# Cached attention decode on one core: two-head units of B against four-head units

## The chip, the cores and the metric

The kernel runs on one NeuronCore of one Trainium2 chip. The metric is the device time of one execution in microseconds (us). The kernel before took 248.0 us, the median of three runs that lie between 247.71 and 248.01. The core has a matrix engine (PE, with its weight loads shown as PEld), a vector engine (DVE), a scalar engine (ACT), a general engine (POOL), a sync engine (SP, which here only issues DMA transfers), and 16 DMA engines that bring data from HBM into the on-chip SBUF.

## The reference

Two independent decode steps, A and B, are computed and concatenated. Each has one query token, 32 query heads, 16 key/value heads of 128 elements and a cache of 8192 positions. A looks at the last 2048 positions alone, B at all of them. All inputs are bf16.

```python
def _B_ref(x, k_cache, v_cache, wq, wo):
    q = (x @ wq).reshape(1, 1, 32, 128).transpose(0, 2, 1, 3)
    k = jnp.repeat(k_cache, 2, axis=1)
    v = jnp.repeat(v_cache, 2, axis=1)
    scores = jnp.einsum("bhqd,bhkd->bhqk", q, k) * (128 ** -0.5)
    p = _softmax(scores, axis=-1)
    o = jnp.einsum("bhqk,bhkd->bhqd", p, v)
    return o.transpose(0, 2, 1, 3).reshape(1, 1, 4096) @ wo
```

A is the same with `k_cache[:, :, 6144:, :]` and `v_cache[:, :, 6144:, :]`. Each cache value is used once, so the work is mostly the reading of some 103 MB.

## The kernel before

**Units.** The heads are worked off in units: four units of four key/value heads for A (numbers 0 to 3), then eight units of two heads for B (numbers 4 to 11). K or V of a unit of A is one transfer of 2048 KB (128 rows of 16 KB, one row for each SBUF partition); of a unit of B it is one transfer of 4096 KB (128 rows of 32 KB). A unit's data is cut into slabs of 2048 elements for each partition, 4 slabs in A and 8 in B.

**The ring.** All large loads go through one SBUF buffer, `ring`, of 72 K elements for each partition. `place` gives each load the next free stretch, starts again at 0 where the load does not fit before the end, and makes the transfer wait for the last user of whatever lay there. A K transfer is last used by the transpose of its last slab (`T<unit>.<slab>`), a V transfer by the last product with it (`V<unit>.<slab>`). All these transfers are issued by SP, in this order and one after the other: the two wq, then K0, K1, V0, K2, V1 and so on (K is one unit ahead of V), and at the end wo of A and wo of B, the latter in six pieces that grow smaller. A transfer that waits holds up all that stand behind it in SP's program.

**A slab of K** is transposed on DVE (`turn`, L368, into one of three buffers `ktb`) and multiplied on PE with the query (`score`, L385, four matmuls), which adds up a PSUM bank of scores for the unit.

**The softmax of a unit** is a chain over engines: `peak` (maximum on DVE, L400, turned on PE, L402), `spread` (maximum over each head on DVE, and its return to all partitions by a matmul on PE, L425), `expo` (a copy on DVE, L431, and the exponential on ACT, L434), `turnp` (the transposes of the result on DVE, L442 for A and L446 for B).

**The product with V** is `pv` (L461), four matmuls of a slab that write to different row groups of one PSUM bank; `take` copies the bank out on ACT, and `fold` (L477) adds the parts on PE.

**Order.** Each engine has its own list, and the order in it is written out: the loop at L485 puts the slabs of unit i+1 (`ahead`) between the steps of the softmax of unit i. In B the last four of the eight slabs of unit i+1 stand between the products of unit i, one slab after every second product. After the loop come the row sums, the division and the product with wo (L544), whose pieces wait for the pieces of wo.

Of the kernel before, what the change touches and what calls it, by code (L numbers as in the profile page):

```python
# [5 lines left out]
F32 = mybir.dt.float32  # L6
# [106 lines left out]
def bass_concat_heads__sliding_block_cached__gqa_block_cached__decode_kernel(nc, A_x, A_k_cache, A_v_cache, A_wq, A_wo,  # L113
# [19 lines left out]
    zb = nc.alloc_sbuf_tensor("zb", [128, NP, 4, ZW], BF16)  # L133
# [6 lines left out]
    mr = nc.alloc_sbuf_tensor("mr", [128, 32], F32)  # L140
    mexpa = nc.alloc_sbuf_tensor("mexpa", [1, 128], F32)
# [4 lines left out]
    mexp = nc.alloc_sbuf_tensor("mexp", [128, 128], F32)  # L146
# [3 lines left out]
    pts = nc.alloc_sbuf_tensor("pts", [128, 16, 16, 2, 2], BF16)  # L150
    rsall = nc.alloc_sbuf_tensor("rsall", [128, NP], F32)
    cls = nc.alloc_sbuf_tensor("cls", [128, 4], F32)
# [65 lines left out]
    kv_at = {}  # L218

    def load_a(kind, u):  # L220
        c = (ks if kind == "K" else vs)[0]
        src = bass.AP(tensor=c.tensor, offset=c.offset + (4 * u * SK + SK - W_A) * DH,
                      ap=[[TA * DH, 32], [SK * DH, 4], [1, TA * DH]])
        kv_at[kind, "A", u] = place(TA * DH, ["T%d.%d" % (u, NA - 1) if kind == "K" else "V%d.%d" % (u, NA - 1)],
                                    lambda e, t: e.dma_start(t, src), "%s%d" % (kind, u))

    def load_b(kind, p):
        c = (ks if kind == "K" else vs)[1]
        src = c[0, 2 * p:2 * p + 2, :, :].rearrange("h (q t) d -> (h q) (t d)", q=64)
        i = NQ + p  # L230
        kv_at[kind, "B", p] = place(ROW, ["T%d.%d" % (i, NB - 1) if kind == "K" else "V%d.%d" % (i, NB - 1)],
                                    lambda e, t: e.dma_start(t, src), "%s%d" % (kind, i))

    UNITS = [("A", u) for u in range(NQ)] + [("B", p) for p in range(NP)]
    NU = len(UNITS)
    for i in range(NU + 1):
        for kind, n in (("K", i), ("V", i - 1)):
            if 0 <= n < NU:
                side, u = UNITS[n]
                (load_a if side == "A" else load_b)(kind, u)  # L240
# [10 lines left out]
    def slab(kind, side, u, s):  # L251
        return kv_at[kind, side, u][:, s * SLAB:(s + 1) * SLAB]
# [9 lines left out]
    op("pool", lambda e: e.memset(mexp[:], 0.0), name="mexp0")  # L262
# [33 lines left out]
    op("dve", lambda e: e.memset(vb[0][:, :], 0.0), name="vb0.0")  # L296
    for h in range(2):
        op("dve", lambda e, h=h: e.tensor_reduce(
            cls[:, 2 * h:2 * h + 2], view(identf, 128, 64 * h, [[1, 2], [32, 2], [2, NB]]), AX.XY, ALU.add),
            deps=["identf"], name="clsB%d" % h)  # L300
# [12 lines left out]
    for P in range(2):  # L313
# [24 lines left out]
        srcs = [[512, NP], [64, 2], [1, 2], [128, 2]]  # L338
        for b in range(4):
            if P == 1:  # L340
                op("dve", lambda e, b=b: e.tensor_copy(
                    view(zb, NP * 4 * ZW, 32 * b + W0, [[4 * ZW, NP], [2 * ZW, 2], [ZW, 2], [1, 2]], 32, 32 * b),
                    view(ktb, KT, b // 2 * 256, srcs, 32, 32 * b)),
                    deps=["qT%d" % u for u in range(8, 16)] + ["zb0"], name="z1.%d" % b)
# [9 lines left out]
    nslab = [NA if side == "A" else NB for side, _ in UNITS]  # L354
# [9 lines left out]
    def turn(i, s):  # L364
        side, u = UNITS[i]
        k = k0[i] + s
        kt, src = ktb[:, (k % NKT) * SLAB:(k % NKT + 1) * SLAB], slab("K", side, u, s)
        op("dve", lambda e: e.transpose(kt.bitcast(I32), src.bitcast(I32)),  # L368
           deps=["K%d" % i] + (["S%d" % (k - NKT)] if k >= NKT else Z), name="T%d.%d" % (i, s))
# [35 lines left out]
    def spread(i):  # L405
        side, _ = UNITS[i]
        deps = ["mT%d" % i, "mexp0"] + (["mx%d" % (i - 1), "bc%d" % (i - 1)] if i else [])
        if side == "A":
            op("dve", lambda e: e.tensor_reduce(mr[0:1, 8:16], view(mb, 512, 0, [[1, 8], [8, 16]], parts=1),
                                                AX.X, ALU.max), deps=deps, name="mr%d" % i)  # L410
            op("dve", lambda e: e.tensor_scalar(
                mexpa[:].rearrange("p (a m) -> p a m", m=8), view(mr, 32, 8, [[0, 16], [1, 8]], parts=1), -SCALE, None,
                ALU.mult), deps=["mr%d" % i], name="mx%d" % i)
        else:
            for h in range(2):
                op("dve", lambda e, h=h: e.tensor_reduce(
                    mr[0:1, 2 * h:2 * h + 2], view(mb, 512, 64 * h, [[1, 2], [32, 2], [2, NB]], parts=1), AX.XY, ALU.max),
                    deps=deps, name="mr%d" % i if h else None)
            for h in range(2):
                op("dve", lambda e, h=h: e.tensor_scalar(  # L420
                    view(mexp, 128, 64 * h, [[32, 2], [2, NB], [1, 2]], parts=1),
                    view(mr, 32, 2 * h, [[0, 2], [0, NB], [1, 2]], parts=1), -SCALE, None, ALU.mult),
                    deps=["mr%d" % i], name="mx%d" % i if h else None)
        row = mexpa if side == "A" else mexp
        op("pe", lambda e: e.matmul(mb[:, 128:129], lhsT=row[0:1, :], rhs=onesf[0:1, 0:1], start=True, stop=True),  # L425
           deps=["mx%d" % i, "ones"], name="bc%d" % i)

    def expo(i):
        side, u = UNITS[i]
        c = i % 2  # L430
        op("dve", lambda e: e.tensor_copy(nb[:, c:c + 1], mb[:, 128:129]),  # L431
           deps=["bc%d" % i] + (["exp%d" % (i - 2)] if i >= 2 else []), name="nb%d" % i)
        acc = (rsa if side == "A" else rsall)[:, u:u + 1]
        op("act", lambda e: e.activation(psb[:, :], sbank[i][:, :], ACT.Exp, bias=nb[:, c:c + 1], scale=SCALE,  # L434
                                         accum_out=acc),
           deps=["nb%d" % i, "warm1"] + (["PT%d" % (i - 1)] if i else []), name="exp%d" % i)

    def turnp(i):
        side, _ = UNITS[i]
        deps = ["exp%d" % i, "pts0"] + (["V%d.%d" % (i - 1, nslab[i - 1] - 1)] if i else [])  # L440
        if side == "A":
            op("dve", lambda e: e.transpose(view(pta, NA * 128, 0, [[8, 16], [128, NA], [1, 8]]), psb[:, :]),  # L442
               deps=deps, name="PT%d" % i)
        else:
            for h in range(2):
                op("dve", lambda e, h=h: e.transpose(  # L446
                    view(pts, 1024, 2 * h, [[4, 16], [64, 16], [1, 2]], 64, 64 * h), psb[64 * h:64 * h + 64, :]),
                   deps=deps, name="PT%d" % i if h else None)

    def pv(i, s):  # L450
        side, u = UNITS[i]

        def mm(e):
            src = slab("V", side, u, s)
            for j in range(4):
                if side == "A":
                    lhsT = pta[:, s, 4 * j:4 * j + 4, :].rearrange("p t k -> p (t k)")
                else:
                    lhsT = view(pts, 1024, 64 * s + 16 * j, [[1, 16]])
                n = 32 if side == "A" else 16  # L460
                ins = e.matmul(vbank[i][32 * j:32 * j + n, :], lhsT=lhsT, rhs=src[:, 512 * j:512 * j + 512],  # L461
                               start=(s == 0), stop=(s == nslab[i] - 1))
            return ins
        op("pe", mm, deps=["V%d" % i, "PT%d" % i, "vb0.0"] + (["xo%d" % (i - 1)] if i else []), name="V%d.%d" % (i, s))
# [20 lines left out]
    for i in range(NU):  # L485
# [34 lines left out]
        lsel[:, 1, :].rearrange("p (g c) -> p g c", c=4), rsall[:, :].unsqueeze(2).to_broadcast([128, NP, 4]),  # L520
        view(cls, 4, 0, [[0, NP], [1, 4]]), ALU.mult), deps=["exp%d" % last, "clsB0", "clsB1"], name="lsel")
# [68 lines left out]
```

## Time and profile before

| what | value |
|---|---|
| median of three runs | 248.0 us (247.71 to 248.01) |
| the profiled execution | 247.88 us |
| its span, first to last instruction | 246.1 us |
| PE busy | 182.6 us (74%) |
| DVE busy | 146.0 us (59%) |
| ACT busy | 23.6 us (10%) |
| read from HBM | 102.76 MB, 418 GB/s over the span |
| mean granted PE clock | 0.826 of full |

The span is what the profile shows; the device time is 1.78 us longer in the profiled execution. Busy shares are means over the whole span. The DMA rows of the page give the mean busy share of the 16 DMA engines in 40 slices of 6.15 us and the rate at which they moved data.

### The profile page before, as it was taken

The page shows a single profiled execution, that of the slowest core. Times are in us where ns is not written, and L with a number is a line of the kernel's source. Part 1 is how long each engine was busy: PE and PEld are TensorE (multiplying, and loading weights), DVE is VectorE, ACT ScalarE, POOL GpSimd, SP SyncE. Part 2 cuts the span into 40 slices and gives each one's busy share as a digit, 9 for nine tenths or more (in the row PEclk, how much of TensorE's full clock was granted, in tenths as well). Part 3 has the DMA queues.
Part 4 walks back from the last instruction along what each step waited for, and adds up shares of the span by engine and source line. Part 5 has one row for each costly group of instructions (what it writes and reads, how often), then busy time and mean ns, then how long its engine had stood idle before and what let it go on. Part 6 is the DMA issues. An engine that isn't in the chain of part 4 may idle for free.

```text
span 246.1 us, 2421 instructions
## 1 busy us (share of the span) xinstructions
PE 182.6 (74%) x1009; PEld 75.8 (31%) x1009; DVE 146.0 (59%) x224; ACT 23.6 (10%) x48; POOL 1.8 (1%) x12
## 2 busy tenths in 40 slices
PE   1169857789868787878759849939949939985695
PEld 0024322234423241252142224215215205231562
DVE  2467877577688687259449447656736826932200
ACT  2002110021111010000001001001001001011000
POOL 2000000000000000000000000000000000000000
PEclk9999995787999977968976965985895985795589
DMA  7999999999999999999999999999999999999993
GB/s 261 423 440 421 442 426 419 426 429 471 426 418 437 426 426 426 423 431 431 431 442 439 431 426 437 442 423 422 426 426 426 437 434 426 431 432 461 389 400 139
DMA packets 5058, 102.91 MB, mean 418 GB/s; under 512 B 564, under 2 KB 824, under 8 KB 1336
## 3 DMA queue, kind: packets, MB, share of 16 engines
q1 hardware_dynamic: 5044, 102.77, 97.8%
q8 instruction: 8, 0.13, 0.2%
q10 hardware_dynamic: 4, 0.00, 0.0%
q14 instruction: 2, 0.02, 0.0%
HBM read 102.76 MB, written 0.00 MB: 418 GB/s over the span
## 4 chain that ended last, share of the span: by engine, by line
DMA 57%; PE 22%; DVE 16%; issue 2%; SPq 1%; ACT 0%; DVEq 0%
DMA ring<-in_B_k_cache_dram 31%; DVE ktb L368 13%; DMA ring<-in_B_v_cache_dram 10%; DMA ring<-in_B_wo_dram 10%; PE qb L385 6%; DMA ring<-in_A_wq_dram 5%; PE sb L324 4%; PE sb L385 4%; PE qb L324 3%; PE ob L477 2%; DVE pts L446 2%; PE mb L425 1%; SPq L247 1%; PE qb L377 1%; PE vb L461 0%
## 5 line engine op out<-in xcount | busy, mean ns | idle before, releaser
L368 DVE STREAM_TRANSPOSE ktb<-ring 128x1024 int32<-128x1024 int32 x80 | 95.3, 1221 | 16.4 <-DMA ring<-in_B_k_cache_dram 13.8
L385 PE MATMUL sb<-ktb,zb 128*128 128x512 bf16 x256 | 83.1, 462 | 25.4 <-DVE ktb L368 25.4
L385 PEld LDWEIGHTS sb<-ktb,zb 128*128 128x128 bf16 x256 | 23.0, 108 | 75.5 <-DVE ktb L368 42.3
L461 PE MATMUL vb<-ring,pts 128*16 128x512 bf16 x256 | 21.1, 420 | 3.9 <-DVE pts L446 2.6
L385 PE MATMUL qb<-ktb,za 128*128 128x512 bf16 x64 | 21.5, 488 | 1.5 <-DVE ktb L368 1.5
L477 PEld LDWEIGHTS ob<-sel,xo 128*128 128x128 f32 x96 | 18.5, 272 | 4.5 <-issue 1.6
L400 DVE TENSOR_REDUCE mx<-sb 128x1 f32<-128x512 f32 x8 | 5.5, 691 | 22.9 <-PE sb L385 22.9
L477 PE MATMUL ob<-sel,xo 128*128 128x4 f32 (+1 forms) x96 | 16.9, 301 | 0.7 <-ACT xo L468 0.7
L468 ACT ACTIVATE xo<-vb 128x512 f32<-128x512 f32 x12 | 7.2, 597 | 91.9 <-PE vb L461 91.9
L324 PE MATMUL sb<-ring,xrep 128*128 128x512 bf16 x40 | 10.6, 418 | 6.6 <-DMA ring<-in_A_wq_dram 5.7
L431 DVE COPY nb<-mb 128x1 f32<-128x1 f32 x12 | 1.9, 159 | 18.2 <-PE mb L425 18.2
L544 PE MATMUL qb<-ring,oP 128*1 128x320 bf16 (+1 forms) x128 | 10.8, 318 | 1.4 <-DMA ring<-in_A_wo_dram 0.7
L446 DVE STREAM_TRANSPOSE pts<-psb 64x512 bf16<-64x512 bf16 x16 | 11.0, 688 | 1.0 <-ACT psb L434 0.8
L434 ACT ACTIVATE psb<-sb,nb 128x512 bf16<-128x512 f32 x8 | 5.5, 687 | 61.1 <-DVE nb L431 61.1
L385 PEld LDWEIGHTS qb<-ktb,za 128*128 128x128 bf16 x64 | 6.4, 115 | 13.8 <-issue 7.0
L335 DVE STREAM_TRANSPOSE ktb<-qsb 128x256 int32<-128x256 int32 x16 | 7.1, 445 | 5.6 <-ACT qsb L330 5.3
L461 PEld LDWEIGHTS vb<-ring,pts 128*16 128x16 bf16 x256 | 4.1, 91 | 18.4 <-issue 15.3
L402 PE MATMUL mb<-identf,mx 128*1 128x128 f32 x24 | 4.6, 271 | 7.0 <-DVE mx L400 7.0
L324 PE MATMUL qb<-ring,xrep 128*128 128x512 bf16 x40 | 9.3, 379 | 0.0
L544 PEld LDWEIGHTS qb<-ring,oP 128*1 128x1 bf16 x128 | 6.6, 90 | 5.5 <-DMA ring<-in_B_wo_dram 2.2
L324 PEld LDWEIGHTS sb<-ring,xrep 128*128 128x128 bf16 x40 | 4.1, 105 | 12.6 <-issue 9.0
L554 DVE CAST outsb<-qb 1x256 bf16<-1x256 f32 x2 | 0.8, 421 | 11.5 <-PE qb L544 11.5
(73 smaller groups left out, 71.5 us busy)
## 6 DMA issues: line engine op xcount, KB each, us to landing
ring<-in_B_k_cache_dram SPq DMA_DIRECT2D x8, 4096.0 KB, 25.2
ring<-in_B_v_cache_dram SPq DMA_DIRECT2D x8, 4096.0 KB, 32.2
ring<-in_A_k_cache_dram SPq DMA_DIRECT2D x4, 2048.0 KB, 31.5
ring<-in_A_v_cache_dram SPq DMA_DIRECT2D x4, 2048.0 KB, 26.8
ring<-in_A_wo_dram SPq DMA_DIRECT2D x1, 4608.0 KB, 16.6
ring<-in_A_wq_dram SPq DMA_DIRECT2D x1, 4096.0 KB, 12.6
ring<-in_B_wq_dram SPq DMA_DIRECT2D x1, 4096.0 KB, 22.6
ring<-in_B_wo_dram SPq DMA_DIRECT2D x1, 2304.0 KB, 21.8
```

The costliest lines, as they stand in the source:

```text
L324: ins = e.matmul(bank[:, :], lhsT=lhsT, rhs=o, start=(k == 0), stop=(k == 4))
L335: op("dve", lambda e, n=n: e.transpose(ktb[:, n * 512:(n + 1) * 512].bitcast(I32), qsb[:, n % 2, :].bitcast(I32)), deps=["qe%d" % u] + ([" ...
L368: op("dve", lambda e: e.transpose(kt.bitcast(I32), src.bitcast(I32)), deps=["K%d" % i] + (["S%d" % (k - NKT)] if k >= NKT else Z), name="T ...
L385: ins = e.matmul(bank[:, :], lhsT=lhsT, rhs=view(ktb, KT, (k % NKT) * SLAB + 64 * c + v, [[128, 16], [2, 32]]), start=(side == "B" and s = ...
L400: op("dve", lambda e: e.tensor_reduce(mx[:, 0:1], sbank[i][:, :], AX.X, ALU.max), deps=["S%d" % (k0[i] + nslab[i] - 1)] + (["mT%d" % (i - ...
L402: op("pe", lambda e: e.matmul(mb[0:1, 0:128], lhsT=mx[:, 0:1], rhs=identf[:, :], start=True, stop=True), deps=["max%d" % i] + was, name="m ...
L434: op("act", lambda e: e.activation(psb[:, :], sbank[i][:, :], ACT.Exp, bias=nb[:, c:c + 1], scale=SCALE, accum_out=acc), deps=["nb%d" % i, ...
L446: op("dve", lambda e, h=h: e.transpose(view(pts, 1024, 2 * h, [[4, 16], [64, 16], [1, 2]], 64, 64 * h), psb[64 * h:64 * h + 64, :]), deps= ...
L461: ins = e.matmul(vbank[i][32 * j:32 * j + n, :], lhsT=lhsT, rhs=src[:, 512 * j:512 * j + 512], start=(s == 0), stop=(s == nslab[i] - 1))
L468: op("act", lambda e: e.activation(xo[:, c, :], vbank[i][:, :], ACT.Copy), deps=["V%d.%d" % (i, nslab[i] - 1)] + (["O%d" % (i - 1)] if i e ...
L477: ins = e.matmul(ob[:, at:at + w], lhsT=xo[:, c, 128 * t:128 * t + 128], rhs=sel[:, w * t:w * t + w], start=(t == 0), stop=(t == 3))
L544: ins = e.matmul(fb[r:r + 1, 0:hi - lo], lhsT=oP[:, P, k0 + k:k0 + k + 1], rhs=wo_at[P, c][:, k * DM + lo:k * DM + hi], start=(k0 + k == 0 ...
```

## The change

B is worked off in four units of four heads (numbers 4 to 7), like A, and no longer in eight units of two. A partition's row of a unit is then 64 KB. V of a unit of B is one transfer of 8192 KB with rows of 64 KB, but for the last unit, where it is two transfers of 4096 KB with half rows. K of a unit of B is two transfers of 4096 KB, each with the first or the second 32 KB of every 64 KB row; the slabs 0 to 7 wait for the first half and 8 to 15 for the second. There is one softmax for four heads, so four in B and not eight. The products of a slab with V have weights of 32 columns and not 16. In the order written out, all slabs of unit i+1 now stand ahead of all products of unit i.

```diff
+    def load_kv(kind, i):
+        side, u = UNITS[i]
+        c = (ks if kind == "K" else vs)["AB".index(side)]
+        use = "T%d.%d" if kind == "K" else "V%d.%d"
...
+        rows = c[0, 4 * u:4 * u + 4, :, :].rearrange("h (q t) d -> (h q) (t d)", q=32)
+        n = 2 if kind == "K" or i == NU - 1 else 1
+        kv_at[kind, i] = []
+        for half in range(n):
+            src = rows[:, half * ROW // n:(half + 1) * ROW // n]
+            kv_at[kind, i].append(place(ROW // n, [use % (i, (half + 1) * NB // n - 1)],
+                                        lambda e, t, src=src: e.dma_start(t, src), "%s%d.%d" % (kind, i, half)))
...
-            for h in range(2):
-                op("dve", lambda e, h=h: e.transpose(
-                    view(pts, 1024, 2 * h, [[4, 16], [64, 16], [1, 2]], 64, 64 * h), psb[64 * h:64 * h + 64, :]),
-                   deps=deps, name="PT%d" % i if h else None)
+            for b in range(4):
+                op("dve", lambda e, b=b: e.transpose(
+                    view(pts, NB * 128, 2 * b, [[8, 16], [128, NB], [1, 2]], 32, 32 * b), psb[32 * b:32 * b + 32, :]),
+                   deps=deps, name="PT%d" % i if b == 3 else None)
...
-        op("pe", mm, deps=["V%d" % i, "PT%d" % i, "vb0.0"] + (["xo%d" % (i - 1)] if i else []), name="V%d.%d" % (i, s))
+        op("pe", mm, deps=[landed, "PT%d" % i] + (["xo%d" % (i - 1)] if i else []), name="V%d.%d" % (i, s))
...
         turnp(i)
-        ahead(1)
-        rest = len(todo)
+        ahead(len(todo))
         for s in range(nslab[i]):
             pv(i, s)
-            if s % 2 and rest:
-                ahead(1)
-        ahead(len(todo))
         take(i)
```

The rest follows from this: the start-up memset of `pts` is twice as long and that of `zb` shorter, that of the V bank is gone, the row sums `rsb` have one column for each unit, and the maxima over the heads of a unit of B take one reduction and one multiplication in place of two and two.

With the new sizes `place` gives these stretches of the ring (in K elements) and waits, in SP's order from the first transfer of B on:

| transfer | stretch | waits for the last use of |
|---|---|---|
| K4 first half | 24 to 40 | wq of B, K0 |
| K4 second half | 40 to 56 | K1, V0 |
| V3 | 56 to 64 | K2 |
| K5 halves | 0 to 16, 16 to 32 | V1 and K3; V2 and the first half of K4 |
| V4 | 32 to 64 | the second half of K4, V3 |
| K6 halves | 0 to 16, 16 to 32 | the halves of K5 |
| V5 | 32 to 64 | V4 |
| K7 halves | 0 to 16, 16 to 32 | the halves of K6 |
| V6 | 32 to 64 | V5 |
| V7 halves | 0 to 16, 16 to 32 | the halves of K7 |
| wo of A | 32 to 50 | V6 |
| wo of B, six pieces | 50 to 68 | transfers long used |

More of the change, by code (lines that the diff above doesn't have):

```diff
@@ L18 @@
 SCALE = DH ** -0.5
-NP = G // 2
 SLAB = 2048
-ROW = 2 * SK // 128 * DH
+NQ = G // 4
+ROW = 4 * SK // 128 * DH
 NB = ROW // SLAB
-NQ = G // 4
 TA = 4 * W_A // 128
@@ L131, in bass_concat_heads__sliding_block_cached__gqa_block_cached__decode_kernel @@
     qsb = nc.alloc_sbuf_tensor("qsb", [128, 2, 512], BF16)
-    zb = nc.alloc_sbuf_tensor("zb", [128, NP, 4, ZW], BF16)
+    zb = nc.alloc_sbuf_tensor("zb", [128, NQ, 4, ZW], BF16)
     za = nc.alloc_sbuf_tensor("za", [128, NQ, 4, ZA], BF16)
@@ L139, in bass_concat_heads__sliding_block_cached__gqa_block_cached__decode_kernel @@
     mx = nc.alloc_sbuf_tensor("mx", [128, 8], F32)
-    mr = nc.alloc_sbuf_tensor("mr", [128, 32], F32)
-    mexpa = nc.alloc_sbuf_tensor("mexpa", [1, 128], F32)
+    mr = nc.alloc_sbuf_tensor("mr", [128, 8], F32)
     pta = nc.alloc_sbuf_tensor("pta", [128, NA, 16, 8], BF16)
@@ L145, in bass_concat_heads__sliding_block_cached__gqa_block_cached__decode_kernel @@
     clsa = nc.alloc_sbuf_tensor("clsa", [128, 8], F32)
-    mexp = nc.alloc_sbuf_tensor("mexp", [128, 128], F32)
+    mexp = nc.alloc_sbuf_tensor("mexp", [1, 128], F32)
     nb = nc.alloc_sbuf_tensor("nb", [128, 4], F32)
     psb = nc.alloc_sbuf_tensor("psb", [128, 512], BF16)
-    pts = nc.alloc_sbuf_tensor("pts", [128, 16, 16, 2, 2], BF16)
-    rsall = nc.alloc_sbuf_tensor("rsall", [128, NP], F32)
-    cls = nc.alloc_sbuf_tensor("cls", [128, 4], F32)
+    pts = nc.alloc_sbuf_tensor("pts", [128, NB, 16, 4, 2], BF16)
+    rsb = nc.alloc_sbuf_tensor("rsb", [128, NQ], F32)
+    clsb = nc.alloc_sbuf_tensor("clsb", [128, 8], F32)
     sel = nc.alloc_sbuf_tensor("sel", [128, 32], F32)
@@ L218, in bass_concat_heads__sliding_block_cached__gqa_block_cached__decode_kernel @@
     kv_at = {}
[L220 to L234, printed above, removed]
-    NU = len(UNITS)
+    UNITS = [(side, u) for side in "AB" for u in range(NQ)]
+    NU = len(UNITS)
+    nslab = [NA if side == "A" else NB for side, _ in UNITS]
+    def load_kv(kind, i):
+        side, u = UNITS[i]
+        c = (ks if kind == "K" else vs)["AB".index(side)]
+        use = "T%d.%d" if kind == "K" else "V%d.%d"
+        if side == "A":
+            src = bass.AP(tensor=c.tensor, offset=c.offset + (4 * u * SK + SK - W_A) * DH,
+                          ap=[[TA * DH, 32], [SK * DH, 4], [1, TA * DH]])
+            kv_at[kind, i] = [place(TA * DH, [use % (i, NA - 1)], lambda e, t: e.dma_start(t, src), "%s%d.0" % (kind, i))]
+            return
+        rows = c[0, 4 * u:4 * u + 4, :, :].rearrange("h (q t) d -> (h q) (t d)", q=32)
[5 more added lines that the diff above has]
+                                        lambda e, t, src=src: e.dma_start(t, src), "%s%d.%d" % (kind, i, half)))
     for i in range(NU + 1):
@@ L238, in bass_concat_heads__sliding_block_cached__gqa_block_cached__decode_kernel @@
             if 0 <= n < NU:
-                side, u = UNITS[n]
-                (load_a if side == "A" else load_b)(kind, u)
+                load_kv(kind, n)
     wo_at = {}
@@ L249, in bass_concat_heads__sliding_block_cached__gqa_block_cached__decode_kernel, with slab @@
             k0 += kk
-    def slab(kind, side, u, s):
-        return kv_at[kind, side, u][:, s * SLAB:(s + 1) * SLAB]
+    def slab(kind, i, s):
+        parts = kv_at[kind, i]
+        per = nslab[i] // len(parts)
+        return parts[s // per][:, s % per * SLAB:(s % per + 1) * SLAB], "%s%d.%d" % (kind, i, s // per)
     op("pool", lambda e: e.memset(onesb[:], 1.0), name="onesb")
@@ L261, in bass_concat_heads__sliding_block_cached__gqa_block_cached__decode_kernel @@
     op("pool", lambda e: e.tensor_copy(identf[:], ident[:]), deps=["ident"], name="identf")
-    op("pool", lambda e: e.memset(mexp[:], 0.0), name="mexp0")
     op("pool", lambda e: e.memset(onesf[:], 1.0), name="ones")
@@ L295, in bass_concat_heads__sliding_block_cached__gqa_block_cached__decode_kernel @@
     op("dve", lambda e: e.memset(pts[:], 0.0), name="pts0")
-    op("dve", lambda e: e.memset(vb[0][:, :], 0.0), name="vb0.0")
-    for h in range(2):
-        op("dve", lambda e, h=h: e.tensor_reduce(
-            cls[:, 2 * h:2 * h + 2], view(identf, 128, 64 * h, [[1, 2], [32, 2], [2, NB]]), AX.XY, ALU.add),
-            deps=["identf"], name="clsB%d" % h)
+    op("dve", lambda e: e.tensor_reduce(clsb[:].rearrange("p (b r) -> p b r", r=2),
+                                        view(identf, 128, 0, [[32, 4], [1, 2], [2, 16]]), AX.X, ALU.add),
+       deps=["identf"], name="clsb")
     op("dve", lambda e: e.tensor_reduce(clsa[:], view(identf, 128, 0, [[1, 8], [8, 16]]), AX.X, ALU.add),
@@ L337, in bass_concat_heads__sliding_block_cached__gqa_block_cached__decode_kernel @@
                 deps=["qe%d" % u] + (["z0.%d" % i for i in range(4)] if P else []), name="qT%d" % u)
-        srcs = [[512, NP], [64, 2], [1, 2], [128, 2]]
         for b in range(4):
@@ L341, in bass_concat_heads__sliding_block_cached__gqa_block_cached__decode_kernel @@
                 op("dve", lambda e, b=b: e.tensor_copy(
-                    view(zb, NP * 4 * ZW, 32 * b + W0, [[4 * ZW, NP], [2 * ZW, 2], [ZW, 2], [1, 2]], 32, 32 * b),
-                    view(ktb, KT, b // 2 * 256, srcs, 32, 32 * b)),
+                    view(zb, NQ * 4 * ZW, 32 * b + W0, [[4 * ZW, NQ], [2 * ZW, 2], [ZW, 2], [1, 2]], 32, 32 * b),
+                    view(ktb, KT, b * 256, [[1024, NQ], [64, 2], [1, 2], [128, 2]], 32, 32 * b)),
                     deps=["qT%d" % u for u in range(8, 16)] + ["zb0"], name="z1.%d" % b)
@@ L351, in bass_concat_heads__sliding_block_cached__gqa_block_cached__decode_kernel @@
     QE = ["qe%d" % u for u in range(16)]
-    nslab = [NA if side == "A" else NB for side, _ in UNITS]
     k0 = [sum(nslab[:i]) for i in range(NU)]
@@ L364, in turn @@
     def turn(i, s):
-        side, u = UNITS[i]
         k = k0[i] + s
-        kt, src = ktb[:, (k % NKT) * SLAB:(k % NKT + 1) * SLAB], slab("K", side, u, s)
+        kt = ktb[:, (k % NKT) * SLAB:(k % NKT + 1) * SLAB]
+        src, landed = slab("K", i, s)
         op("dve", lambda e: e.transpose(kt.bitcast(I32), src.bitcast(I32)),
-           deps=["K%d" % i] + (["S%d" % (k - NKT)] if k >= NKT else Z), name="T%d.%d" % (i, s))
+           deps=[landed] + (["S%d" % (k - NKT)] if k >= NKT else Z), name="T%d.%d" % (i, s))
     def score(i, s):
@@ L405, in spread @@
     def spread(i):
[L406 to L425, printed above, removed]
+        A = UNITS[i][0] == "A"
+        deps = ["mT%d" % i] + (["mx%d" % (i - 1), "bc%d" % (i - 1)] if i else [])
+        rows = [[1, 8], [8, 16]] if A else [[32, 4], [1, 2], [2, 16]]
+        out = mr[0:1, :] if A else mr[0:1, :].rearrange("p (b r) -> p b r", r=2)
+        op("dve", lambda e: e.tensor_reduce(out, view(mb, 512, 0, rows, parts=1), AX.X, ALU.max), deps=deps,
+           name="mr%d" % i)
+        to, of = ([[8, 16], [1, 8]], [[0, 16], [1, 8]]) if A else ([[32, 4], [2, 16], [1, 2]], [[2, 4], [0, 16], [1, 2]])
+        op("dve", lambda e: e.tensor_scalar(view(mexp, 128, 0, to, parts=1), view(mr, 8, 0, of, parts=1), -SCALE, None,
+                                            ALU.mult), deps=["mr%d" % i], name="mx%d" % i)
+        op("pe", lambda e: e.matmul(mb[:, 128:129], lhsT=mexp[0:1, :], rhs=onesf[0:1, 0:1], start=True, stop=True),
            deps=["mx%d" % i, "ones"], name="bc%d" % i)
@@ L432, in expo @@
            deps=["bc%d" % i] + (["exp%d" % (i - 2)] if i >= 2 else []), name="nb%d" % i)
-        acc = (rsa if side == "A" else rsall)[:, u:u + 1]
+        acc = (rsa if side == "A" else rsb)[:, u:u + 1]
         op("act", lambda e: e.activation(psb[:, :], sbank[i][:, :], ACT.Exp, bias=nb[:, c:c + 1], scale=SCALE,
@@ L444, in turnp @@
         else:
-            for h in range(2):
-                op("dve", lambda e, h=h: e.transpose(
-                    view(pts, 1024, 2 * h, [[4, 16], [64, 16], [1, 2]], 64, 64 * h), psb[64 * h:64 * h + 64, :]),
-                   deps=deps, name="PT%d" % i if h else None)
+            for b in range(4):
+                op("dve", lambda e, b=b: e.transpose(
+                    view(pts, NB * 128, 2 * b, [[8, 16], [128, NB], [1, 2]], 32, 32 * b), psb[32 * b:32 * b + 32, :]),
+                   deps=deps, name="PT%d" % i if b == 3 else None)
     def pv(i, s):
-        side, u = UNITS[i]
+        src, landed = slab("V", i, s)
         def mm(e):
-            src = slab("V", side, u, s)
             for j in range(4):
-                if side == "A":
+                if UNITS[i][0] == "A":
                     lhsT = pta[:, s, 4 * j:4 * j + 4, :].rearrange("p t k -> p (t k)")
                 else:
-                    lhsT = view(pts, 1024, 64 * s + 16 * j, [[1, 16]])
-                n = 32 if side == "A" else 16
-                ins = e.matmul(vbank[i][32 * j:32 * j + n, :], lhsT=lhsT, rhs=src[:, 512 * j:512 * j + 512],
+                    lhsT = view(pts, NB * 128, 128 * s + 32 * j, [[1, 32]])
+                ins = e.matmul(vbank[i][32 * j:32 * j + 32, :], lhsT=lhsT, rhs=src[:, 512 * j:512 * j + 512],
                                start=(s == 0), stop=(s == nslab[i] - 1))
             return ins
-        op("pe", mm, deps=["V%d" % i, "PT%d" % i, "vb0.0"] + (["xo%d" % (i - 1)] if i else []), name="V%d.%d" % (i, s))
+        op("pe", mm, deps=[landed, "PT%d" % i] + (["xo%d" % (i - 1)] if i else []), name="V%d.%d" % (i, s))
     def take(i):
@@ L472, in fold @@
         side, u = UNITS[i]
-        c, w, at = (1, 8, 8 * u) if side == "A" else (0, 4, HQ + 4 * u)
+        c, at = (1, 8 * u) if side == "A" else (0, HQ + 8 * u)
         def mm(e):
             for t in range(4):
-                ins = e.matmul(ob[:, at:at + w], lhsT=xo[:, c, 128 * t:128 * t + 128], rhs=sel[:, w * t:w * t + w],
+                ins = e.matmul(ob[:, at:at + 8], lhsT=xo[:, c, 128 * t:128 * t + 128], rhs=sel[:, 8 * t:8 * t + 8],
                                start=(t == 0), stop=(t == 3))
@@ L519, in bass_concat_heads__sliding_block_cached__gqa_block_cached__decode_kernel @@
     op("dve", lambda e: e.tensor_tensor(
-        lsel[:, 1, :].rearrange("p (g c) -> p g c", c=4), rsall[:, :].unsqueeze(2).to_broadcast([128, NP, 4]),
-        view(cls, 4, 0, [[0, NP], [1, 4]]), ALU.mult), deps=["exp%d" % last, "clsB0", "clsB1"], name="lsel")
+        lsel[:, 1, :].rearrange("p (u m) -> p u m", m=8), rsb[:, :].unsqueeze(2).to_broadcast([128, NQ, 8]),
+        view(clsb, 8, 0, [[0, NQ], [1, 8]]), ALU.mult), deps=["exp%d" % last, "clsb"], name="lsel")
     op("pe", lambda e: e.matmul(mb[:, 0:64], lhsT=onesf[:, :], rhs=lsel[:].rearrange("p c k -> p (c k)"),
```

## The prediction

> **What bounds the kernel now.** I read the page's DMA rows and its chain of waits first, then the transfers' times to landing, then the windows by stage, and last SP's timeline, because a kernel that reads everything once should be held by its transfers.
>
> ```profile
> span 246.1 us, 2421 instructions
> ...
> DMA  7999999999999999999999999999999999999993
> GB/s 261 423 440 421 442 426 419 426 429 471 426 418 437 426 426 426 423 431 431 431 442 439 431 426 437 442 423 422 426 426 426 437 434 426 431 432 461 389 400 139
> DMA packets 5058, 102.91 MB, mean 418 GB/s; under 512 B 564, under 2 KB 824, under 8 KB 1336
> ...
> q8 instruction: 8, 0.13, 0.2%
> ...
> DMA 57%; PE 22%; DVE 16%; issue 2%; SPq 1%; ACT 0%; DVEq 0%
> ...
> ring<-in_B_k_cache_dram SPq DMA_DIRECT2D x8, 4096.0 KB, 25.2
> ring<-in_B_v_cache_dram SPq DMA_DIRECT2D x8, 4096.0 KB, 32.2
> ```
>
> All 16 DMA engines are busy in every slice but the first and the last, at about 430 GB/s. A transfer of B takes 25 to 32 us from issue to landing, although 4.19 MB at 430 GB/s are 9.75 us: it stands behind two others. So "DMA 57%" in the chain is a queue that is always filled, and the 38% of PE and DVE in it only say what let the next transfer be issued. The windows say it by stage (columns: window and length; busy time and count of PE, PEld, DVE, ACT, POOL; granted clock; DMA share; GB/s):
>
> ```profile
> 96.00:124.50 28.50, 21.95 (x122) 7.66 (x118) 14.21 (x19) 1.97 (x4) 0.00 (x0) 0.82 1.01 435
> 124.50:163.40 38.90, 29.70 (x152) 11.65 (x152) 23.73 (x33) 2.75 (x6) 0.00 (x0) 0.78 1.00 430
> 163.40:202.20 38.80, 30.23 (x152) 11.74 (x152) 23.80 (x32) 2.75 (x6) 0.00 (x0) 0.77 1.00 429
> ...
> 240.00:244.00 4.00, 3.30 (x37) 1.45 (x33) 0.00 (x0) 0.00 (x0) 0.00 (x0) 1.00 0.55 205
> ```
>
> DMA is full while PE has 30 of 39 us to do and DVE 24. Only in the last 4 us is half of the DMA time empty.
>
> The trace's packet records (start, size and duration of each) give the price of a transfer. One row is one packet: median 613 ns for 16384 bytes, 1216 for 32768, 1368 for 36864. So 16384 more bytes cost 603 ns, and a row costs 613 - 603 = 10 ns besides. A transfer ends with a 4-byte packet of 9 ns on each engine. Each engine carries 8 rows of a transfer, and the transfers of B end 9.715 us apart on every engine: 8 x 1.213 (the shortest) + 0.009 = 9.713. Nothing is lost between them.
>
> **The change, part by part.**
>
> *Packets.* Three V transfers (V4, V5, V6) get rows of 64 KB. A row then costs 10 + 4 x 603 = 2422 ns and not 2 x 1216 = 2432. On each engine 3 x 8 = 24 rows save 24 x 0.010 = 0.24 us, and three end packets less 0.03, together 0.27. If a 64 KB row is cut in two, 0.03 is left. The other end: rows of A, whose neighbours stand 2 MB apart in HBM, average 619 ns against 611 for the shortest, 1.3% more. Should 64 KB spacing do this to the 67 MB of B (16 x 9.715 = 155 us), it would be +2.0. I take -0.27, by the straight line through the three sizes. A rule speaks against it: the Trainium skill's "DMA: Bandwidth & Descriptors", "Latency and other measured facts", says rows at a large power-of-two pitch slow a copy, 207 GB/s at 512 KiB and 164 at 2 MiB against 214. Rows of A at 2 MB run at full rate here. Were 64 KB to cost the 3% of its 512 KiB figure, it would be an estimated +4.7 us. The same page's "Anatomy of one DMA" gives a fixed 2.0 us for each DMA, which would make three fewer transfers worth an estimated -6 us; landings 9.715 us apart leave no room for that.
>
> *Does the queue stay filled?* B's V now has one region, 32 to 64 K, so each V must be used up before the next is issued, and K halves alternate in 0 to 32 K. I compare each issue with the moment the first DMA engine runs out. In the packet records the first engine ends V2 at 58.51, a 4096 KB transfer takes 9.715 and a 2048 KB one 4.89. So in the new order it ends K4's first half at 68.2, the second at 77.9, V3 at 82.8, K5 at 92.5 and 102.2, V4 at 121.6, K6 at 131.3 and 141.0. Issues of before, on SP:
>
> ```profile
> 52.70 0.54 SPq L225 DMA_DIRECT2D ring<-in_A_v_cache_dram  x1
> 61.33 0.33 SPq L232 DMA_DIRECT2D ring<-in_B_k_cache_dram  x1
> 70.10 0.33 SPq L232 DMA_DIRECT2D ring<-in_B_v_cache_dram  x1
> 82.85 0.33 SPq L232 DMA_DIRECT2D ring<-in_B_k_cache_dram  x1
> ```
>
> K4's second half waits for the products with V0, which end at 54.8 (started 53.70, 16 matmuls in 1.05); needed by 68.2. V3 stands behind it and waits for K2's last transpose, 61.3 (82.8 - 4.9 = 77.9). K5's first half waits for K3's, 70.1 (82.8); its second for slab 7 of K4, 82.8 (92.5). All this is the work of before.
>
> V4 is the tight one: slabs 8 to 15 of K4 and the moved products of unit 3 come first.
>
> ```profile
> 71.05 1.05 PE L461 MATMUL vb<-ring,pta 128*32 128x512 bf16 x16
> ...
> 77.07 5.71 DVE L368 STREAM_TRANSPOSE ktb<-ring 128x1024 int32<-128x1024 int32 x5
> ...
> 78.33 1.05 PE L385 MATMUL sb<-ktb,zb 128*128 128x512 bf16 x4 [0.67 <-DVE ktb L368]
> ```
>
> Five transposes take 5.71, 1.14 each, and a slab's four matmuls 1.05, so DVE sets the pace: 82.8 + 8 x 1.14 = 91.9, the last score 93.0, the 16 products 1.05: V4 issued at 94.1. From issue to first packet takes 1.04 (the first transfer: 0.73 to 1.77). Needed by 102.2; 7 us are left.
>
> Then a steady round. The last engine ends 2.4 us after the first, and the waiting instruction starts 0.45 later (K5: 85.21, DVE at 85.68). V4 lands at 124.4. Its 64 matmuls, PE cold (32 of them took 3.59 at 223.79), take 7.2: V5 issued at 131.6, needed by 141.0. K6 lands at 134.1. From the first transpose of a unit to its fourth the softmax chain takes 7.9 (105.09 to 112.97); four transposes of `pts` in place of two (0.69 each, the count of elements in a row being the same) add 1.4, and slabs 3 to 7 5.75: K7's first half can be issued at 149.2, needed by 160.4. A round is 2 x 9.715 + 19.35 = 38.8 us of DMA against 16 x 1.14 + 9.3 + 7.2 = 35 us of this chain, and nothing slips further. These costs I put at nothing; DMA hides them while the V region is given back 9 us ahead, and past that each us counts in full. Four softmaxes fewer are hidden likewise. Start-up memsets lie before 33 us, ahead of the first wait for K.
>
> *The end.* wo of A waits for V6: landed 201.9 + 7.2 = 209.1, needed by 218.6. V7's second half lands at 221, like V11 before (221.2); its 8 slabs take 3.59, and from their end to the division's last step took 4.8 before: 229.4, ahead of wo's landing at 232.1. The end stays with wo's pieces.
>
> *Instruction loads.* The page's eight packets on q8 stop a DMA engine for 1.55 us each, on eight different engines. The first, at 37.96, hits the engine already last (+0.86 becomes +2.39), and this engine ends at 243.30, where the first ends at 240.96. It comes before any changed instruction, so I expect it unmoved. PE ran 2018 instructions; four softmaxes and folds fewer are 4 x 24 = 96 less, and the last load (241.45, at instruction 1998 with weight loads and waits) should vanish, which costs and gains nothing while the first decides. Bounds: -1.5 (the late engine is spared) to +1.55 (hit twice). I take 0.
>
> **Sum:** -0.27. The profiled execution was 247.88 with span 246.1; the span becomes 245.8, the execution 247.6. It lay 0.12 under the median, so the median becomes 247.7.
>
> **The rivals.**
> *V4 comes late* (slower). If PE runs cold from 77 to 95, a slab takes 1.70 to 1.89 (such rows stand at 106.39), the twelve slabs 4 to 15 take 6.7 to 9.0 more and the products 0.7: issue at 101.5 to 103.8, first packet 102.6 to 104.9, so 0.4 to 2.7 idle: 248.1 to 250.4. It decides from an issue after 101.2. For it: one V region. Against: the clock row was full from 62 to 89, and denser work leaves fewer pauses.
> *Strided or 64 KB rows are slow:* -0.03 + 2.0 gives 250. For it: rows of A are 1.3% longer. Against: wo's rows of 36864 bytes lie on the line.
> *The instruction loads fall differently* (faster): 0.3 to 1.5 us less at the end, 246.2 to 247.4. For it: fewer PE instructions. Against: the first load's place.
> *The rows are cut in two*, so the change of packets is none: 248.0.
>
> **How the numbers follow.** About 0.2%, 0.5 us, is what a measurement of this kernel can tell from no change. The forecast with the cut rows is "the same", 0.74, and covers 247.4 to 248.3; V4 late 0.06 and slow rows 0.08 make slower 0.14; the instruction loads make faster 0.12. The range 247.1 to 249.0 takes in the near parts of both sides.
>
> **What would show it.** Right: landings of B's 4096 KB still 9.715 apart, 64 KB packets of 2.42 us, every middle slice of DMA at 9, V4's issue near 94, fewer q8 packets. Wrong: a gap in the DMA row near 102 or once in 39 us, or packets off the line.

## The result, and the profile after

The changed kernel takes 247.57 us (median of 22 runs, 247.38 to 247.70), the kernel before, run beside it, 247.86 us (22 runs, 247.57 to 248.06). The ratio is 0.9987, with a 95% interval of 0.9982 to 0.9993: 0.29 us less, 0.13%. The span of the profiled execution fell from 246.1 to 245.8 us. By the prediction's bound of about 0.2% this is no change, though a small gain is there.

The page of the changed kernel, the lines that answer to those shown of before: span; busy share of DMA and its rate in 40 slices; packets; instruction loads; the chain of waits by engine; transfers of B's K.

```profile
span 245.8 us, 2270 instructions
...
DMA  7999999999999999998999999899999999999993
GB/s 256 427 453 422 431 429 428 427 427 464 427 424 392 467 427 427 440 480 384 411 437 435 480 416 501 373 411 424 432 453 459 396 405 424 432 438 462 393 400 134
DMA packets 4625, 102.90 MB, mean 419 GB/s; under 512 B 516, under 2 KB 776, under 8 KB 1288
...
q8 instruction: 7, 0.11, 0.2%
...
DMA 70%; PE 18%; DVE 9%; SPq 1%; issue 1%; ACT 0%; DVEq 0%
...
ring<-in_B_k_cache_dram SPq DMA_DIRECT2D x8, 4096.0 KB, 25.8
```

The queue is as full as before. The rate jumps more from slice to slice (384, 501, 373) only because a packet's bytes are put in the slice in which it starts, and a packet of 64 KB is long; the two 8s in the DMA row lie between slices at 9 and go with this. There are 432 fewer packets of data and transfer ends, and one fewer on q8. The chain now has 70% DMA and half as much DVE, yet the time is nearly the same: how the chain names a full queue changed, not what bounds the kernel.

The windows of the changed kernel, in the same stretches (window and length; busy time and count of PE, PEld, DVE, ACT, POOL; granted clock; DMA share; GB/s):

```profile
96.00:124.50 28.50, 17.76 (x78) 6.27 (x82) 21.61 (x24) 0.78 (x2) 0.00 (x0) 0.98 1.02 439
124.50:163.40 38.90, 27.66 (x144) 10.28 (x148) 22.23 (x24) 1.38 (x3) 0.00 (x0) 0.80 1.00 431
163.40:202.20 38.80, 27.19 (x144) 10.81 (x140) 22.35 (x24) 1.38 (x3) 0.00 (x0) 0.77 1.00 432
240.00:244.00 4.00, 3.09 (x34) 1.36 (x32) 0.17 (x1) 0.18 (x1) 0.00 (x0) 1.00 0.46 174
```

PE, DVE and ACT have a little less to do in a round, and DMA moves 431 to 432 GB/s where it moved 429 to 430. In the last window DMA's share is 0.46 and not 0.55, because the last bytes come a little earlier.

SP's timeline of the changed kernel (start, length, line, transfer) has the issues that were worked out:

```profile
95.29 0.33 SPq L236 DMA_DIRECT2D ring<-in_B_v_cache_dram  x1
...
130.84 0.33 SPq L236 DMA_DIRECT2D ring<-in_B_v_cache_dram  x1
149.26 9.34 SPq L236 DMA_DIRECT2D ring<-in_B_k_cache_dram  x2
...
207.17 0.33 SPq L248 DMA_DIRECT2D ring<-in_A_wo_dram  x1
```

These are V4, V5, K7's halves and wo of A. In the packet records the first DMA engine runs out at 102.42, 141.19, 160.54 and 218.74, so each issue is 7 to 12 us ahead, and the first packet follows an issue by some 1 us. A 64 KB row is one packet, median 2422 ns, and V4 takes 121.77 - 102.42 = 19.35 us on the first engine.

### The profile page after: what moved, and what is told of

Its sections match the earlier page's. It is cut to its first block, busy times and chain, and to the rows that moved or that the text cites. A ratio compares the mean times of both kernels' runs of the same rounds, so it can differ in the third digit from the quotient of the medians.

```text
span 245.8 us, 2270 instructions
## 1 busy us (share of the span) xinstructions
PE 166.4 (68%) x961; PEld 68.7 (28%) x961; DVE 139.2 (57%) x190; ACT 18.1 (7%) x36; POOL 1.7 (1%) x11
## 2 busy tenths in 40 slices
DMA packets 4625, 102.90 MB, mean 419 GB/s; under 512 B 516, under 2 KB 776, under 8 KB 1288
## 4 chain that ended last, share of the span: by engine, by line
DMA 70%; PE 18%; DVE 9%; SPq 1%; issue 1%; ACT 0%; DVEq 0%
DMA ring<-in_B_v_cache_dram 39%; DMA ring<-in_B_wo_dram 14%; DMA ring<-in_B_k_cache_dram 12%; DVE ktb L367 8%; PE vb L448 7%; DMA ring<-in_A_wq_dram 5%; PE sb L325 4%; PE qb L325 3%; PE sb L384 1%; SPq L248 1%; PE qb L384 1%; PE ob L464 1%; DVE ktb L336 0%; DVE zb L341 0%; DVE qsb L334 0%
## 5 line engine op out<-in xcount | busy, mean ns | idle before, releaser
L384 PE MATMUL sb<-ktb,zb 128*128 128x512 bf16 x256 | 74.6, 427 | 24.7 <-DVE ktb L367 21.6
L448 PE MATMUL vb<-ring,pts 128*32 128x512 bf16 x256 | 24.0, 551 | 21.7 <-DMA ring<-in_B_v_cache_dram 17.6
L384 PE MATMUL qb<-ktb,za 128*128 128x512 bf16 x64 | 17.5, 406 | 3.3 <-DVE ktb L367 3.3
L448 PEld LDWEIGHTS vb<-ring,pts 128*32 128x32 bf16 x256 | 8.6, 129 | 36.2 <-DMA ring<-in_B_v_cache_dram 20.0
L455 ACT ACTIVATE xo<-vb 128x512 f32<-128x512 f32 x8 | 4.8, 598 | 132.6 <-PE vb L448 132.6
L464 PEld LDWEIGHTS ob<-sel,xo 128*128 128x128 f32 x64 | 10.9, 244 | 4.0 <-ACT xo L455 2.4
L435 DVE STREAM_TRANSPOSE pts<-psb 32x512 bf16<-32x512 bf16 x16 | 11.1, 695 | 1.0 <-ACT psb L423 0.8
L464 PE MATMUL ob<-sel,xo 128*128 128x8 f32 x64 | 10.1, 285 | 1.2 <-ACT xo L455 1.2
L325 PEld LDWEIGHTS sb<-ring,xrep 128*128 128x128 bf16 x40 | 4.1, 105 | 12.5 <-issue 9.1
L409 DVE TENSOR_REDUCE mr<-mb 1x8 f32<-1x128 f32 x8 | 1.9, 242 | 8.1 <-PE mb L401 8.1
L399 DVE TENSOR_REDUCE mx<-qb 128x1 f32<-128x512 f32 x4 | 2.8, 691 | 5.3 <-PE qb L384 5.3
## 6 DMA issues: line engine op xcount, KB each, us to landing
ring<-in_A_wq_dram SPq DMA_DIRECT2D x1, 4096.0 KB, 12.5
```

The source lines that it names most:

```text
L325: ins = e.matmul(bank[:, :], lhsT=lhsT, rhs=o, start=(k == 0), stop=(k == 4))
L384: ins = e.matmul(bank[:, :], lhsT=lhsT, rhs=view(ktb, KT, (k % NKT) * SLAB + 64 * c + v, [[128, 16], [2, 32]]), start=(side == "B" and s = ...
L399: op("dve", lambda e: e.tensor_reduce(mx[:, 0:1], sbank[i][:, :], AX.X, ALU.max), deps=["S%d" % (k0[i] + nslab[i] - 1)] + (["mT%d" % (i - ...
L409: op("dve", lambda e: e.tensor_reduce(out, view(mb, 512, 0, rows, parts=1), AX.X, ALU.max), deps=deps, name="mr%d" % i)
L435: op("dve", lambda e, b=b: e.transpose(view(pts, NB * 128, 2 * b, [[8, 16], [128, NB], [1, 2]], 32, 32 * b), psb[32 * b:32 * b + 32, :]), ...
L448: ins = e.matmul(vbank[i][32 * j:32 * j + 32, :], lhsT=lhsT, rhs=src[:, 512 * j:512 * j + 512], start=(s == 0), stop=(s == nslab[i] - 1))
```

## The experiments

Twelve kernels were run, each of them the changed kernel with one edit. Their ratios are to the kernel before on the same chip.

**Undo the rows alone.**

```diff
-        n = 2 if kind == "K" or i == NU - 1 else 1
+        n = 2
```

> The changed kernel, but V of units 4 to 6 comes in two transfers of 32 KB half rows like K. Theory (rows): 24 rows of 64 KB on each engine become 48 of 32 KB, so +0.24 us for the rows and +0.03 for three end packets: 247.8, level with the kernel before (ratio to it 1.000), no packets of 65536 bytes, V's halves 9.71 us apart. Rival (the gain comes from fewer PE instructions, fewer instruction loads and four softmaxes less): all of that is kept here, so 247.6, ratio 0.9988.

Measured: 247.71 us, ratio 0.9998 (0.9989 to 1.0007); the first engine ends V5's halves 9.71 us apart. That is where the theory put it, but the interval overlaps that of the changed kernel (0.9982 to 0.9993), so this time alone does not settle it.

**More rows.** The same with 4 in place of 1 for the V of units 4 to 6 (and other names for the transfers, since two would have coincided).

> The changed kernel, but V of units 4 to 6 comes in four transfers of 16 KB quarter rows. Theory (rows): a V takes 32 x 0.611 + 4 x 0.009 = 19.59 us on each engine where 8 x 2.418 + 0.009 = 19.35 stood; three of them +0.71: 248.3, ratio to before 1.0017. Rival (not the rows): 247.6, ratio 0.9988.

Measured: 248.22 us, ratio 1.0018 (1.0009 to 1.0026), where 1.0017 was expected. Its page has the packets:

```profile
span 246.6 us, 2277 instructions
...
DMA packets 5921, 102.90 MB, mean 417 GB/s; under 512 B 660, under 2 KB 920, under 8 KB 1432
```

The instructions of PE, DVE and ACT are the same as in the changed kernel and the bytes are too; only the packets went from 4625 to 5921. With 24, 48 and 96 rows of V on each engine the ratio is 0.9987, 0.9998 and 1.0018. Rows that cost some 10 ns each explain all three; fewer softmaxes or PE instructions explain none of the differences, since all three have them.

The landings show it without the noise of whole executions. In the packet records one DMA engine leads, ending each transfer first, and no instruction load hits it. From its end of the first wq transfer to its end of wo of A it takes 217.647 us in the kernel before, 217.361 in the changed kernel, 217.614 with half rows and 218.064 with quarter rows. Against before, the prices of rows and end packets give -0.27, -0.03 and +0.44 us; these landings give -0.29, -0.03 and +0.42.

**The order of before.** Eight slabs of unit i+1 stand between the products of unit i again:

```diff
-        ahead(len(todo))
+        ahead(1)
+        rest = len(todo)
         for s in range(nslab[i]):
             pv(i, s)
+            if s % 2 and rest:
+                ahead(1)
+        ahead(len(todo))
```

> The changed kernel with the order of before: of the 16 slabs of unit i+1 four go ahead, eight stand between the products of unit i, one after every second product, and four behind. Theory (a product that waits for V holds the scores behind it, their transposes and so the issue of the next K): slab 7 of unit 5 comes only after V4 has landed, K6's first half can be issued at 127 and its first packet is ready at 128, where the queue runs out at 121.8: 6 us lost; the second half, behind slab 15, some 5 more; three such rounds make 247.6 + 25 to 35. Rival (the order is free, since PE and DVE are hidden by DMA): 247.6.

Measured: 278.11 us, ratio 1.1224 (1.1175 to 1.1273), +30 us. The DMA row of this kernel's page and SP's timeline (K6's first half, V5, K7's first half):

```profile
DMA  7999999999999999944969977295999729789994
```

```profile
128.17 12.81 SPq L236 DMA_DIRECT2D ring<-in_B_k_cache_dram  x2
141.03 0.43 SPq L236 DMA_DIRECT2D ring<-in_B_v_cache_dram  x1
177.82 13.52 SPq L236 DMA_DIRECT2D ring<-in_B_k_cache_dram  x2
```

K6's first half is issued at 128.17, 6.5 us after the first engine ran out at 121.63, and its second half 12.5 us later. Three rounds of digits under 9 follow. So with these units and this ring the new order of slabs and products is needed, and the large V region would be a loss without it.

**Delay the release of V: products made again.** After each group of four products in units 4 to 6:

```diff
+            for _ in range(N):
+                for j in range(4):
...
+                    ins = e.matmul(vb[1][32 * j:32 * j + 32, :], lhsT=lhsT, rhs=src[:, 512 * j:512 * j + 512],
+                                   start=True, stop=True)
             return ins
```

N = 1:

> The changed kernel with the products with V of units 4 to 6 made a second time into an unused PSUM bank (the second result is not read). 64 warm matmuls in groups of four took 4.2 us, so V5 is issued 4.2 us later, at 135, and its first packet is ready at 136; the first DMA engine runs out at 141.2. Theory (the queue has this slack): 247.6, no change beyond 0.2. Rival (PE's chain sets the pace of B): three times 4.2, 260.

Measured: 248.74 us (247.85 to 249.06), ratio 1.0037 (1.0028 to 1.0046). A miss for both: 1.2 us more than the changed kernel by the medians (0.9 in the profiled executions), not 0 and not 12.6. No gap opened, and the last of the 16 engines ended wo of A at 231.77 against 231.86 in the changed kernel. The time went after that: an instruction load (a packet on q8) falls at 241.86, and the last packet of wo lands at 243.81 and not 243.04.

N = 3:

> The same with the products made four times. The release of a V region moves by 3 x 4.2 = 12.6 us: V5 issued at 143.4, first packet at 144.5, 3.3 after the first engine has run out at 141.2. The same at V6 and at wo of A, which wait for V5 and V6. Theory (slack of about 9 us, then each us counts): +9.9, 257.5, with three gaps in the DMA row. Rival (PE sets the pace): 3 x 12.6 = +38, 285. Rival (V's region does not matter): 247.6.

Measured: 249.00 us, ratio 1.0045 (1.0031 to 1.0058), far below 257.5. V5 was issued at 140.86, sooner than expected, since 64 warm matmuls more take 3.5 us (repeat groups of twelve 0.65 apart) and not 4.2. But even so its data was late for the first engine: it ended V5 at 161.65, not 160.4. The last engine ended V5 at 162.71, where the changed kernel has 162.74. The delay of 1.2 us fell on the engines that were ahead and not on the one that decides. The 1.4 us came later: the last engine ended the next V transfer 1.0 us and wo of A 1.35 us after the changed kernel's.

**Which of the two is it, the products or the loads?** N = 1, 1 and 2 in units 4, 5 and 6, so that the last instruction load falls at the same place of PE's program as in the changed kernel:

> The changed kernel with the products with V of units 4 and 5 made once more and of unit 6 twice more (not read): 256 more matmuls with their weight loads, 512 instructions, two instruction loads more, so that the last load falls at the same place of PE's program as in the changed kernel (236 us), where products made twice put it at 241.9, under the last pieces of wo. Theory (the 0.9 us of the doubled products came from that late load; the products themselves are hidden): 247.6. Rival (the products cost the time): 64 matmuls more than there, so at least 248.7.

Measured: 248.84 us, ratio 1.0039 (1.0024 to 1.0054): by the number alone the rival's result. The trace speaks against it. V5 and V6 were issued in time (132.48, 172.33), the last engine ended wo of A at 231.81, and only wo's small pieces were late: one engine ended the last of them at 244.19. The load at 236.3 had hit an engine that was late already; the spread between the first and the last engine went from 2.39 to 2.78 us with it. So the place of a load is not enough; it matters which engine it hits. The next run takes the products away and keeps the loads.

```diff
+    def idle(e):
+        for _ in range(256):
+            ins = e.matmul(ob[:, 511:512], lhsT=onesb[0:1, :], rhs=onesb[0:1, 0:1], start=True, stop=True)
+        return ins
+    op("pe", idle, deps=["onesb"], name="idle")
```

> The changed kernel with 256 empty matmuls (one column, not read) on PE before the first wait for wq, where PE is idle for 12 us, and no product more. That is 512 instructions, two instruction loads more, both early, and the later ones at the same places of PE's program: nine loads in all, as with 1, 1 and 2 more products, which gave 248.84. Theory (there the loads and the DMA engines that they hit cost the time, the products none): the end moves here too, 248.2 to 249.2, and the trace shows wo's last pieces held by one engine that was hit twice. Rival (the products cost it): 247.6. A third outcome, 247.6 with nine loads on nine engines, would leave open which engine a load hits.

Measured: 248.69 us, ratio 1.0034 (1.0021 to 1.0048), with no product more. The empty matmuls did hold up PE's first products (17.76 and not 14.62 us), but not the queue: the last engine ended wo of A at 231.57, no later than the 231.86 of the changed kernel. The last packet of wo lands at 244.19, the same as with 1, 1 and 2 products. The last instructions of this kernel (first) and of the changed kernel (second), from the timelines (start, length, engine, line):

```profile
241.83 3.11 PE L533 MATMUL qb<-ring,oP 128*1 128x320 bf16 x32 [0.50 <-DMA ring<-in_B_wo_dram]
244.98 0.43 ACT L541 ACTIVATE outsb<-qb 1x320 bf16<-1x320 f32 x1 [5.10 <-PE qb L533]
```

```profile
240.66 1.25 PE L527 MATMUL qb<-ring,oP 128*1 128x320 bf16 x16 [0.48 <-DMA ring<-in_B_wo_dram]
242.06 1.72 PE L527 MATMUL qb<-ring,oP 128*1 128x320 bf16 x16
243.82 0.43 ACT L535 ACTIVATE outsb<-qb 1x320 bf16<-1x320 f32 x1 [4.84 <-PE qb L527]
```

PE's last products wait for wo's pieces, and the copy out starts 1.16 us later. The two extra loads lie at 13.8 and 21.1 us, 220 us before the time is lost. The load at 236.3 is the ninth here and with the 1, 1 and 2 products, and it hits a late engine; at 236.1 in the changed kernel it is the seventh, and it hits one of the early ones. Why it hits another engine is not shown.

**Larger gaps.** N = 3, 3 and 2, and N = 5, 5 and 2, in units 4, 5 and 6:

> The same with 3, 3 and 2 more (512 matmuls, four instruction loads more, the last at the same place). V5 issued at 141, first packet at 142, where the first DMA engine has run out at 141.1 and the last at 143.3. Theory (only the engine that is last decides; a gap that it does not see costs nothing at once, but the engines start V5 together, and the instruction loads after it count again): 248.5 to 249.1. Rival A (each us after the first engine's end counts): 247.6 + 0.9 at V5, 248.5, with the skew between the engines kept at V5. Rival B (the skew absorbs it for good): 247.6.

> The same with 5, 5 and 2 more (768 matmuls, six loads more). A repeat of 64 warm matmuls takes 3.46 us, so V5 is issued at 147.8, first packet 148.8, 7.7 after the first engine and 5.5 after the last has run out; V6 after another gap of 6.5; wo of A without one. Theory: wo of A lands some 13 us later, 258 to 263, two gaps in the DMA row. Rival (a gap is made up later): under 252.

Measured: 248.82 us, ratio 1.0042 (1.0027 to 1.0057), and 259.99 us, ratio 1.0489 (1.0468 to 1.0510); both where the theory put them. With 3, 3 and 2 the last engine ends V5 at 162.36, no later than the 162.74 of the changed kernel, and the 16 engines then lie 0.52 us apart where they lay 2.20. Loads at 163.5 and later spread them to 1.84 again at the next transfer, whose last engine is 0.9 us late: the gap had used up the lead of the other engines. The first number alone would also fit a loss at V5, up to some tenths; the landings show where it arose. With 5, 5 and 2 the DMA row has its two gaps and wo of A lands at 244.24, 12.4 us late:

```profile
DMA  8899999999999999999998097999968999999993
```

**V4, the tight place.** The products of unit 3 made 9, 8 and 16 times more:

> The changed kernel with the products of unit 3, the last of A, made nine times more into an unused PSUM bank (not read): 9 x 1.05 = 9.45 us ahead of V4's issue. It was issued at 95.29 and needed by 102.42 (the first engine's end of the transfer before); now issue at 104.7, first packet 105.8, 3.4 us of empty queue. Theory: +3.4, 251.0, ratio to before 1.012. Rival (V4 has more slack than counted, or the queue is refilled otherwise): 247.6.

> The changed kernel with the products of unit 3 made eight times more (128 matmuls, 6.9 us at 54 ns; one instruction load more, the last at the same place). V4's issue, seen between 92.5 and 95.3, goes to 99.4 to 102.2, the first packet to 100.4 to 103.2; the first DMA engine runs out at 102.4, the last at 104.5. Theory (the last engine decides): 247.5 to 247.9. Rival (the slack of V4 is smaller than counted): 249 and more.

> The products of unit 3 made sixteen times more (256 matmuls, 13.8 us, two instruction loads more). V4 issued between 106.3 and 109.1, first packet 107.3 to 110.1, where the last DMA engine has run out at 104.5. Theory (past the last engine's end each us counts, and the loads after it count again): +2.8 to +5.6 for the gap and about 1 for the loads, 251 to 254. Rival (V4's lateness is made up later, since the queue is deep in B): 247.6.

Measured: 9 times, 248.68 us (247.78 to 249.99), ratio 1.0046 (1.0023 to 1.0068); 8 times, 247.58 us (247.34 to 249.23), ratio 1.0001 (0.9985 to 1.0017); 16 times, 254.30 us (253.58 to 255.05), ratio 1.0272 (1.0252 to 1.0292). The first missed its 251: the matmuls took 54 ns and not 66 each, V4 was issued at 100.99 in the profiled execution, and the executions of this kernel scatter over 2 us, as could be at the edge of the slack. V4's issue in the three profiled executions (8, 9 and 16 times, from SP's timelines):

```profile
101.50 0.33 SPq L236 DMA_DIRECT2D ring<-in_B_v_cache_dram  x1
```

```profile
100.99 0.33 SPq L236 DMA_DIRECT2D ring<-in_B_v_cache_dram  x1
```

```profile
107.07 0.33 SPq L236 DMA_DIRECT2D ring<-in_B_v_cache_dram  x1
```

With 16 the gap is in the windows of that kernel:

```profile
96.00:102.00 6.00, 6.00 (x116) 2.97 (x112) 0.31 (x1) 0.00 (x0) 0.00 (x0) 1.00 1.02 434
102.00:108.00 6.00, 6.00 (x102) 2.89 (x91) 0.74 (x3) 0.60 (x1) 0.00 (x0) 1.00 0.06 25
108.00:114.00 6.00, 3.28 (x19) 1.76 (x17) 5.54 (x8) 0.78 (x2) 0.00 (x0) 1.00 1.25 494
```

V4 was issued at 107.07; the first engine had run out at 102.22, the last at 104.32. PE is busy through the whole window, DMA 6% of it. The last engine ended V4 at 129.52 where 123.67 would have followed without a gap, 5.85 us later; the last packet of wo came 5.9 us later than in the changed kernel. Nothing is made up afterwards. The 8 times leave the median where it was, though three of ten executions took 1.0 to 1.7 us more, among them the profiled one (248.90). So the changed kernel has some 6 us of slack here (95.29 to 101.50); where exactly it ends these runs do not show.

## Why the prediction was right

**The packets.** Sized right. A 64 KB row was put at 2422 ns, and its median is 2422; V's transfer at 19.35 us, and it is 19.35. The sum was -0.27 us, the result -0.29 (0.9982 to 0.9993, so 0.17 to 0.45 us). The three row sizes of V give the dose. That a 64 KB row might be cut in two, or cost 1.3% more, is refuted by the same number. The 1.3% itself was misread: the rows of A average 615 ns in the records, not 619, and eight of them pass an engine in 4.89 us, 0.611 each, so A's spacing costs nothing.

The prediction also carried the Trainium skill's figures for row pitches ("DMA: Bandwidth & Descriptors", "Latency and other measured facts"; the smallest slow pitch there is 512 KiB) down to 64 KB, for an estimated +4.7 us. At 64 KB the trace shows no such loss: half rows of K at this pitch have the median of 1216 ns that contiguous rows had. No run tried a larger pitch with long rows, and A is no test of it, since only four neighbouring rows stand 2 MB apart before the next four follow 16 KB on. The fixed 2.0 us in the same page's "Anatomy of one DMA" stands there for DMAs that the general engine issues; SP issues these, and their landings 9.71 us apart leave no room for it.

**The queue.** Right: no gap, and issues at 95.29, 130.84, 149.26 and 207.17 against 94.1, 131.6, 149.2 and 209.1. The softmax's four transposes take 695 ns each, as taken. The costs put at nothing cost nothing up to wo of A, by the landings. What hid them is shown by the delays: issuing V4 6 us later leaves the median where it was, issuing it 12 us later costs 6.7.

**Where the slack ends.** Here a step was wrong. I let each us count from the moment the first engine runs out (102.2 for V4). It is the last engine that decides, 2.0 to 2.3 us later in these runs. So a short gap brings the engines together and its price is not the gap: with 3, 3 and 2 more products nothing at V5, and then what single delays spread anew, about 1 us. The rival "V4 comes late" did not occur. Its prices rested on this step, and they do not fit: the issue at 101.50 would have cost 0.4 us by it, and that execution took 248.9.

**The instruction loads.** The effect on the sum was taken as 0 and is about 0, but by luck, as far as the runs show, and not for the reason given. Seven loads came and not eight, as counted. The first, at 38.2, did not hit the latest engine: it took an engine from +0.26 to +1.81. The second, at 69.0, hit the engine that had started as the latest (+0.64), which became +2.20. So in both kernels the last engine at wo of A is one that ended its first transfer at about 12.95 and was then hit once, and its end moved from 232.11 to 231.86, about what the rows give. "Comes before any changed instruction, so unmoved" was no argument. The bound of about 1.5 us was of the right size: a kernel with two more loads and no product more lost 1.1 us.

**Faster rival.** Not seen. Fewer PE instructions did remove a load, and no time is left over for it.

## What to carry to other kernels

When every DMA engine is busy from the first packet to the last, sum packets and not instructions: bytes at the engine's rate, plus the small price of each row, and check by hand that each transfer is still issued before the queue runs dry. Larger buffers change who releases them, so look at the order of the work that frees them before their size: here the old order with the new buffers cost 30 us, and the longer rows brought 0.3. The last of the parallel engines sets both the end and the slack.

## What was not expected of the hardware

**Instruction loads slow single DMA engines.** A load of 16 KB on q8 came for every 256 PE instructions added: 512, 1024 and 1536 more gave 9, 11 and 13 loads for 7. In the records of the kernels before and after such a packet takes 1.02 to 1.11 us, one engine's data waits for it, and the next data packet on that engine is some 0.5 us longer, together about 1.55 us. The other engines do not take over its rows: the engine that went to +1.81 at 38.2 still stands at +1.83 at 102.4. A gap in the queue evened the engines out (with 3, 3 and 2 more products). Two loads more cost 1.1 us (247.57 to 248.69) with the last engine's end of wo of A no later.

**Loads are not the only such delay.** In the kernels before and after one engine loses about 1 us twice with no packet on q8 to account for it, at 40.84 and 168.25 us before and at 41.32 and 193.45 after; the data packet there is 0.66 us too long. The other traces have such packets too. So of the eight engines that are late at wo of A in the kernel before, seven were hit by a load and the eighth by these two delays. What they are, no run shows.

**Which engine a load hits is open.** In the kernel before the first seven loads delayed seven engines (the eighth came at 241.45, among wo's last pieces); in others a seventh or a ninth load hit an engine that was late already. The time with two loads more was steady from run to run (248.52 to 248.79 in five runs), but what chooses the engine was not found.
